# One more of 24 head pairs through TensorE in single precision, in an attention and gated-MLP kernel whose order of work is a searched table

## The chip, the cores and the metric

The kernel runs on one core of a Trainium2 chip. The metric is device time in microseconds (us) for one launch. Beside the timed runs one execution was recorded by the hardware profiler; all rows below come from that execution. Engines: PE is TensorE (its weight loads are PEld), DVE is VectorE, ACT is ScalarE, POOL is GpSimd, SP is SyncE, which here issues every DMA.

## The reference

Four batches of 12 heads, 448 tokens, 64 channels a head; then a gated MLP with a mixing step over tokens.

```python
scores = scale * np.matmul(q, k.transpose(0, 1, 3, 2))        # causal mask
attn = softmax(scores)
x = np.matmul(attn, v)                                        # heads side by side: 768 columns
h = np.maximum(x @ w_in, 0.0); u, v = h[..., :512], h[..., 512:]
v_s = np.einsum('ts,bsd->btd', w_spatial, layernorm(v)) + b_spatial[None, :, None]
out = (u * v_s) @ w_out
```

## The kernel before, in words

Two heads make a pair, so there are 24 pairs, six a batch. For each pair the kernel loads q and k, turns them so that the 64 channels lie on partitions, multiplies them (the scores), takes the row extreme with the mask (DVE, lines 970 and 1110), the exponential (ACT, 980 and 1129), the row sums and reciprocals, turns the weights, and multiplies by v (line 1255, into the bank `px`). After the sixth pair of a batch `ffn` runs the MLP on TensorE (line 1473).

There are two ways to do a pair, chosen by `TURNED` and `SINGLE`; both hold pairs 0 to 9 before the change.

**A turned pair** (`WIDE`) stays in single precision. q and k come by four loads, one for each of q, k and head (line 701). TensorE turns q and k (line 764, eight transposes) and ACT or DVE copies the result to `qkT`. `wide` makes the scores in three TensorE steps: heads 0 and 1 side by side on the upper and lower 64 rows (`both(0)`, `both(2)`, then `last()`; line 934, sixteen instructions in all). The weights are evened by one scaled copy each (line 1012, seven of them), turned by sixteen TensorE transposes (line 1021), and copied to `et` (seven copies, line 1050).

**A split pair** cuts every operand into a high and a low half-precision part. q and k come by two loads (line 708). ACT sums their squares (line 567), TensorE adds these over partitions (line 604), DVE makes a power of two of it, three engines make the parts (lines 513 to 521), a DMA transpose turns them (line 828), and two copies bring halves across partitions (line 847). The scores are 28 half-precision matmuls in four groups (lines 1101 and 1102). ACT makes the high part of the weights (line 1205), DVE the low part (line 1211), four DMA transposes turn them (line 1229), and the product with v takes three terms, 24 matmuls instead of 16 instructions.

**Pair 0** is turned in a form of its own (`HEADWISE`): line 738 turns q and k once for each head, four copies instead of two follow (lines 747 and 749), and the first four score steps are one head each (`one(g)`).

**Order.** Nothing is scheduled at run time. `Plan.add` numbers the steps in the order in which the Python code makes them. `ORDER` lists these numbers in the order in which they are issued, each engine taking its own from the list; `WHERE` has one letter for each step that may run on more than one engine. An engine works strictly in this order, so a step that waits holds up all behind it on its engine. `plan.run` puts short filler matmuls (line 689) on TensorE early on where it expects a wait. The buffers that tie engines together are four score banks `ps`, three `qk`, two `qkT`, two `e` and two `et`.

Of the kernel before, what the change touches and what calls it, by code (L numbers as in the profile page):

```python
# [12 lines left out]
AF = mybir.ActivationFunctionType  # L13
# [6 lines left out]
HEAD_PE = 690, 680  # L20
HEADWISE = frozenset({0})
# [4 lines left out]
TURNED = frozenset(range(10))  # L26

SINGLE = frozenset(range(10))
# [21 lines left out]
    "AAADAAPPADAPPAPPPAPAAPDAAPAAPPAAPDPAPADDAPAADAAAPAAAPADDDAADAADAPDDDPAADAAPPAAAPDAPAPDAAADPADAPADDPAPDAAPPAAPD"  # L50
    "AAPADAPADPAPAPAPPAPAPPPPPPPAPAPADPPDAPPADPDPAPAPAPPPPAADAAAPAAADPPPPAPAPAPDDAADAAAAPDAPPDAPAPAPDAAPPDDAADAPAPA"
    "PADDAADDDAADADDAAAAAPPADSSAAAAADPDAAAAAPAAPDAADDDPDAPDAPSSPPDPPAPPDPAAAPAAAAAPPPAPAPDDDDADDAADPAPPAPADPADPAAPP"
    "SPPPPPPPPDPADPPDPADPPPDPPDDPPPAPDDPAPPPPDAPPAAPPPAPAADAPPPPPPAPAPAAAAAAAADAAPPPPDDPDPPSPPPDDDAPSPAPPPDPPSSPAAP"
    "PDPPPPADPPDDPADPPDDAADADPPPADAPPDDAAADDDA"
)
ORDER = (
# [243 lines left out]
def kernel(  # L300
# [415 lines left out]
    def qk_turn(p):  # L716
# [3 lines left out]
        if not WIDE[p]:  # L720

            def clear(e):

                if not blank.get(at(t).name):
                    nc.gpsimd.memset(q32(at(t)), 0.0)
                    blank[at(t).name] = True

            plan.add({"POOL": 819}, clear, [], [(t, (0, 0)), (t, (0, 1))])
        if p in HEADWISE:
            pts = [Buf("ps"), Buf("ps")]  # L730
            for h in range(2):
                for n in range(2):
# [1028 lines left out]
```

## Time and profile before

| | |
|---|---|
| median of three timed runs | 358.56 us (358.33 to 358.65) |
| the profiled execution, its own time | 360.6 us |
| its span, first to last instruction | 358.6 us |
| granted TensorE clock over the span | 0.998 |
| PE, PEld, DVE, ACT, POOL busy | 97%, 63%, 80%, 75%, 45% |
| filler matmuls, line 689 | 32, 7.4 us busy |

The profiled execution lies 2.0 us above its span and 2.0 us above the median of the timed runs. A time is read here as a difference to the execution before. A busy share counts an engine as busy from the start of an instruction to its modelled end. In the chain of waits the time of a group of matmuls runs from its first start to the start of what follows.

### The profile page before, as it was taken

What the parts mean: (1) busy time and instruction counts of PE and PEld (TensorE: products, weight loads), DVE (VectorE), ACT (ScalarE), POOL (GpSimd) and SP (SyncE); (2) the same over time, 40 slices, a digit from 0 to 9 for tenths busy, and PEclk for the clock granted to TensorE, in tenths of its full rate; (3) what the DMA queues carried; (4) which work ended last, traced back from release to release, by engine and by line L of the source; (5) the groups of instructions that cost most, each with busy time, mean ns of one, the idle gap of its engine ahead of it and who ended that gap; (6) DMA issues with size and microseconds to landing.
All of it is one profiled execution on the core that took longest, in us unless ns stands there. A gap on an engine that the chain in (4) does not pass through costs nothing.

```text
span 358.6 us, 8098 instructions
## 1 busy us (share of the span) xinstructions
PE 346.2 (97%) x2602; PEld 225.5 (63%) x2602; DVE 285.9 (80%) x1116; ACT 268.7 (75%) x767; POOL 161.6 (45%) x223
## 2 busy tenths in 40 slices
PE   6999899999999999999999999999999999999995
PEld 5476555665555556765455579755755885555695
DVE  4899889999999999889898998987989994263420
ACT  3698899999999999888799989748789684231101
POOL 3133664337656468364374572334686710042400
PEclk9999999999999999999999999999999999999999
DMA  7959979746768999999997898997767978300014
GB/s 162 210 164 242 244 170 215 174 100 166 150 166 186 208 237 181 178 182 139 188 180 153 172 225 162 205 174 156 164 116 156 159 111 174 82 2 0 3 47 130
DMA packets 160796, 55.84 MB, mean 156 GB/s; under 512 B 155249, under 2 KB 156530, under 8 KB 160754
## 3 DMA queue, kind: packets, MB, share of 16 engines
q1 hardware_dynamic: 160754, 55.33, 74.5%
q8 instruction: 20, 0.33, 0.4%
q14 instruction: 22, 0.18, 0.1%
HBM read 26.76 MB, written 5.51 MB: 90 GB/s over the span
## 4 chain that ended last, share of the span: by engine, by line
PE 65%; DMA 10%; DVE 8%; ACT 7%; POOL 4%; issue 3%; SPq 2%; POOLq 0%; ACTq 0%; DVEq 0%
PE pf L1473 43%; PE px L1255 6%; DMA qkT<-qks 4%; PE ps L1021 3%; PE ps L934 3%; PE ps L1101 3%; ACT e L982 3%; PE ps L1102 2%; DMA et<-e 2%; PE ps L764 2%; POOL qks L523 2%; DVE ps L972 1%; DMA o<-in_moe_w_out_dram 1%; DMA wst<-wb 1%; ACT e L489 1%
## 5 line engine op out<-in xcount | busy, mean ns | idle before, releaser
L1473 PE MATMUL pf<-wi,xT 128*128 128x512 f16 (+1 forms) x360 | 61.6, 338 | 0.0
L1473 PE MATMUL pf<-xT,wi 128*128 128x448 f16 x288 | 59.3, 353 | 0.4 <-ACT hv L1536 0.4
L1124 ACT ACTIVATE ps<-ps,sm 128x384 f32<-128x384 f32 (+4 forms) x98 | 45.4, 463 | 13.2 <-DVE sm L1112 8.0
L1473 PE MATMUL pf<-wo,g 128*128 128x384 f32 x288 | 54.9, 341 | 0.0
L1213 DVE SCALAR_TENSOR_TENSOR e<-ps,sm,e 128x256 f16<-128x256 f32 (+4 forms) x98 | 46.3, 505 | 6.3 <-ACT e L489 6.3
L1473 PEld LDWEIGHTS pf<-wo,g 128*128 128x128 f32 x288 | 49.8, 188 | 2.0 <-issue 1.1
L489 ACT ACTIVATE e<-ps,sm 128x256 f16<-128x256 f32 (+4 forms) x98 | 44.3, 509 | 5.5 <-DVE sm L1146 1.9
L1112 DVE CUSTOM_DVE_ANT_0 ps<-ps,mask,sc 128x256 f32<-128x256 f32 (+4 forms) x98 | 47.2, 506 | 1.4 <-PE ps L1102 0.8
L1473 PEld LDWEIGHTS <-wi 128*128 128x128 f16 x288 | 27.4, 98 | 26.7 <-issue 3.0
L1473 PEld LDWEIGHTS <-xT 128*128 128x128 f16 (+1 forms) x360 | 27.2, 103 | 25.4 <-issue 4.7
L491 POOL TENSOR_SCALAR e<-e,sm 128x384 f32<-128x384 f32 (+3 forms) x43 | 23.8, 566 | 41.5 <-ACT e L982 13.6
L982 ACT ACTIVATE e<-ps,sm 128x256 f32<-128x256 f32 (+3 forms) x70 | 34.3, 500 | 4.6 <-DVE sm L972 2.6
L1473 PE MATMUL pf<-wst,vn 128*128 128x448 f16 (+1 forms) x176 | 36.0, 353 | 0.1
L523 POOL TENSOR_TENSOR qks<-qk,qks 112x512 f16<-112x512 f32 x21 | 24.2, 1157 | 20.3 <-ACT qks L489 8.9
L934 PE MATMUL ps<-qkT 64*128 64x128 f32 (+3 forms) x160 | 28.5, 444 | 0.9 <-ACT e L982 0.7
L1102 PE MATMUL ps<-qkT 128*64 128x256 f16 (+4 forms) x196 | 26.3, 284 | 0.4 <-DVE qkT L847 0.4
L1473 PEld LDWEIGHTS <-vn 128*128 128x128 f16 (+1 forms) x176 | 16.8, 98 | 15.2 <-issue 0.5
L1101 PE MATMUL ps<-qkT 128*64 128x256 f16 (+4 forms) x196 | 24.8, 291 | 0.9 <-DVE e L1213 0.7
L972 DVE CUSTOM_DVE_ANT_0 ps<-ps,e 128x128 f32<-128x128 f32 (+2 forms) x60 | 24.3, 441 | 1.2 <-PE ps L934 1.0
L1021 PE MATMUL ps<-ident,e 128*128 128x128 f32 x160 | 23.8, 279 | 1.3 <-POOL e L491 0.5
L1563 POOL TENSOR_TENSOR ln<-ln,mhalf 128x1 f32<-128x1 f32 (+1 forms) x16 | 10.6, 666 | 31.5 <-DVE ln L1555 26.8
L1021 PEld LDWEIGHTS ps<-ident,e 128*128 128x128 f32 x160 | 17.6, 141 | 9.1 <-issue 3.3
(168 smaller groups left out, 729.5 us busy)
## 6 DMA issues: line engine op xcount, KB each, us to landing
wb<-in_moe_w_in_dram SPq DMA_DIRECT2D x12, 512.0 KB, 4.3
vnat<-in_v_dram SPq DMA_DIRECT2D x24, 192.0 KB, 3.9
out_dram<-o SPq DMA_DIRECT2D x12, 384.0 KB, 3.0
qk<-in_k_dram SPq DMA_DIRECT2D x14, 224.0 KB, 4.0
qk<-in_q_dram SPq DMA_DIRECT2D x14, 224.0 KB, 4.2
o<-in_moe_w_out_dram SPq DMA_DIRECT2D x8, 384.0 KB, 4.1
qk<-in_q_dram SPq DMA_DIRECT2D x20, 112.0 KB, 4.8
qk<-in_k_dram SPq DMA_DIRECT2D x20, 112.0 KB, 3.6
```

What stands on the lines that cost most here:

```text
L489: nc.scalar.activation(out=dst, in_=src, func=AF.Copy, scale=scale)
L523: lambda e: HANDLE[e].tensor_tensor(out=dst_l(), in0=src(), in1=dst_h(), op=ALU.subtract),
L934: nc.tensor.matmul(out=at(bank)[r0:r0 + rn, o0:o0 + n], lhsT=flat32(t)[rows, q0:q0 + rn], rhs=k32(t)[rows, :n], start=True, stop=True, ski ...
L972: lambda e, ps=ps, n=n, u=u0 + u, sm=sm, o0=o0, h=h: nc.vector.tensor_tensor_reduce(out=at(ps)[:, o0:o0 + n], in0=at(ps)[:, o0:o0 + n], in ...
L982: lambda e, ps=ps, n=n, u=u0 + u, sm=sm, o0=o0, c=c: nc.scalar.activation(out=at(eb)[:, 128 * c:128 * c + n], in_=at(ps)[:, o0:o0 + n], fu ...
L1021: nc.tensor.transpose(out=at(pt)[:, 128 * i:128 * i + 128], in_=e32(at(eb))[:, c0 + i, :], identity=ident)
L1101: nc.tensor.matmul(out=o, lhsT=w, rhs=qkT[:, 2 + x, :n], start=True, stop=False)
L1102: nc.tensor.matmul(out=o, lhsT=w, rhs=qkT[:, 4 + x, :n], start=False, stop=True)
L1112: lambda e, ps=ps, n=n, u=u, sm=sm, o0=o0, m0=m0: nc.vector.tensor_tensor_reduce(out=at(ps)[:, o0:o0 + n], in0=at(ps)[:, o0:o0 + n], in1=m ...
L1124: nc.scalar.activation(out=dst, in_=src, func=AF.Exp, scale=-1.0, bias=at(sm)[:, u:u + 1], accum_out=at(sm)[:, 4 + 2 * u:5 + 2 * u],)
L1213: lambda e, part=part, src=src, sm=sm, u=u: nc.vector.scalar_tensor_tensor(out=part(1), in0=src(), scalar=at(sm)[:, 12 + u:13 + u], in1=pa ...
L1473: nc.tensor.matmul(out=o, lhsT=a(), rhs=rhs, start=(n0 + n == 0), stop=(n0 + n == len(mms) - 1), skip_group_check=len(out_ap()) > 1,)
```

## The change

Pair 10 becomes a turned pair. Pair 0 loses its own form: the head-by-head turns, copies and score steps are deleted, and it takes those of the other turned pairs. `WHERE` and `ORDER` are replaced (the plan has 2470 steps instead of 2496; only the first line of each table is shown). Constants and all other code stay.

```diff
-HEAD_PE = 690, 680
-HEADWISE = frozenset({0})
...
-TURNED = frozenset(range(10))
-
-SINGLE = frozenset(range(10))
+TURNED = frozenset(range(11))
+
+SINGLE = frozenset(range(11))
...
 WHERE = (
-    "AAADAAPPADAPPAPPPAPAAPDAAPAAPPAAPDPAPADDAPAADAAAPAAAPADDDAADAADAPDDDPAADAAPPAAAPDAPAPDAAADPADAPADDPAPDAAPPAAPD"
...
+    "DADPPDADAAPDPPAAPAPPADPAAAPPDDPAPAPAAAPAAAADADDAPAPADDDAADAADAADDDDAAPAAAAADAPDAPAAAPAAAPAADAPDDPAPAAAPPAAPDAA"
...
 ORDER = (
-    10, 1, 5, 0, 3, 73, 8, 6, 72, 100, 2, 75, 74, 4, 9, 14, 12, 11, 15, 96, 13, 26, 97, 22, 98, 93, 7, 16, 148, 18,
...
+    96, 11, 1, 0, 8, 4, 71, 5, 9, 10, 68, 3, 69, 7, 150, 2, 13, 12, 14, 70, 22, 15, 88, 92, 6, 73, 89, 93, 16, 18,
...
-        if p in HEADWISE:
-            pts = [Buf("ps"), Buf("ps")]
-            for h in range(2):
-                for n in range(2):
...
-        for g in range(4 if p in HEADWISE else 0):
...
-            if p in HEADWISE and n < 2:
-                continue
```

The numbers 10 to 13 are pair 0's loads (q of head 0, q of head 1, k of head 0, k of head 1) in both tables. Pair 1's loads are 72 to 75 before and 68 to 71 after. On TensorE the old table begins 14, 96, 98, 16, 18, 20, 101 (turn of pair 0, two of pair 1, three of pair 0, first scores of pair 0), the new one 14, 92, 16, 94, 97 (turns of pairs 0, 1, 0, 1, first scores of pair 0). The products with v come in the order of pairs 9, 10, 12, 11, 13 before and 9, 12, 11, 10, 13 after.

## Rows read from the trace of the kernel before

**Rows 1.** The page: busy time, share of the span, instructions of each engine.

```profile
PE 346.2 (97%) x2602; PEld 225.5 (63%) x2602; DVE 285.9 (80%) x1116; ACT 268.7 (75%) x767; POOL 161.6 (45%) x223
```

**Rows 2.** Stretches: length, then busy us of PE, PEld, DVE, ACT, POOL.

```profile
50.00:120.00 70.00, 69.40 (x518) 41.10 (x517) 66.03 (x268) 68.32 (x199) 38.88 (x54) 1.00 0.73 170
120.00:180.00 60.00, 57.65 (x450) 36.16 (x448) 53.78 (x220) 53.24 (x158) 30.63 (x39) 1.00 1.01 187
180.00:310.00 130.00, 129.97 (x1051) 88.43 (x1049) 108.69 (x433) 100.56 (x283) 61.67 (x72) 1.00 0.85 163
```

**Rows 3.** Waits of TensorE: total us, times, longest us.

```profile
PE ps L1101 <- DVE e L1213: 0.7, 2, 0.3
...
PE ps L1102 <- DVE qkT L847: 0.4, 1, 0.4
```

**Rows 4.** Chain of waits in order of time: start us, us, what.

```profile
50.59 0.77 PE ps L764 x8
51.36 1.42 PE ps L1021 x13
...
54.16 1.62 PE ps L934 x10
...
59.78 1.75 PE ps L934 x12
61.53 2.03 PE px L1255 x16
...
186.04 6.92 PE pf L1473 x36
...
196.64 0.34 PE px L604 x2
198.80 1.43 PE px L1255 x24
```

**Rows 5.** Timeline of PE: a split pair's first score matmuls, and what follows.

```profile
196.91 0.22 PE L1101 MATMUL ps<-qkT 128*64 128x64 f16 x2
...
198.63 1.54 PE L1255 MATMUL px<-et,vs 128*64 128x448 f16 x20
```

**Rows 6.** Timeline of PE: one group of scores between output matmuls.

```profile
141.07 2.35 PE L1473 MATMUL pf<-wo,g 128*128 128x384 f32 x12
143.35 0.38 PE L1101 MATMUL ps<-qkT 128*64 128x448 f16 x2
...
143.85 5.50 PE L1473 MATMUL pf<-wo,g 128*128 128x384 f32 x30
```

**Rows 7.** Timeline of PE: pair 0's last turn and first scores.

```profile
8.88 0.77 PE L738 MATMUL ps<-ident,qk 112*128 112x112 f32 x4
...
9.69 2.38 PE L934 MATMUL ps<-qkT 64*128 64x128 f32 x12
```

**Rows 8.** Timeline of ACT: a copy of a turned operand, and the first exponential.

```profile
8.40 0.53 ACT L785 ACTIVATE qkT<-ps 128x448 f32<-128x448 f32 x1
...
11.78 0.37 ACT L982 ACTIVATE e<-ps,sm 128x128 f32<-128x128 f32 x1 [2.29 <-DVE sm L972]
```

**Rows 9.** Timeline of SP: issue of the seventh and eighth load.

```profile
3.90 0.49 SPq L701 DMA_DIRECT2D qk<-in_q_dram  x1
4.43 0.49 SPq L701 DMA_DIRECT2D qk<-in_k_dram  x1
```

**Rows 10.** DMA issues up to 12 us: count, KB each, median us to landing.

```profile
qk<-in_k_dram SPq DMA_DIRECT2D x5, 112.0 KB, 3.0
```

**Rows 11.** Groups of ACT by line: count, busy us, mean ns, idle before.

```profile
L489 ACT ACTIVATE e<-ps,sm 128x256 f16<-128x256 f32 (+4 forms) x98 | 44.3, 509 | 5.5 <-DVE sm L1146 1.9 <-DMA et<-e 1.5 <-ACT ps L1124 1.4
...
L1045 ACT ACTIVATE et<-ps 128x384 f32<-128x384 f32 (+3 forms) x47 | 19.1, 446 | 1.7 <-PE ps L1021 1.3 <-DVE et L1047 0.3
```

**Rows 12.** Groups of DVE by line, the same columns.

```profile
L1213 DVE SCALAR_TENSOR_TENSOR e<-ps,sm,e 128x256 f16<-128x256 f32 (+4 forms) x98 | 46.3, 505 | 6.3 <-ACT e L489 6.3
```

**Rows 13.** Timeline of PE: pair 4's k turn waits for its load.

```profile
39.58 0.57 PE L764 MATMUL ps<-ident,qk 112*128 112x112 f32 x4 [1.01 <-DMA qk<-in_k_dram]
```

More of the change, by code (lines that the diff above doesn't have):

```diff
@@ L49 @@
 WHERE = (
-    "AAADAAPPADAPPAPPPAPAAPDAAPAAPPAAPDPAPADDAPAADAAAPAAAPADDDAADAADAPDDDPAADAAPPAAAPDAPAPDAAADPADAPADDPAPDAAPPAAPD"
[L51 to L54, printed above, removed]
+    "DADPPDADAAPDPPAAPAPPADPAAAPPDDPAPAPAAAPAAAADADDAPAPADDDAADAADAADDDDAAPAAAAADAPDAPAAAPAAAPAADAPDDPAPAAAPPAAPDAA"
+    "PDAAPADPDPAPAPDADADPPAPPPADAPAAPPDAAPADPDPAADPAPPPPAADAAAPAAAAPPPDAPAPPPDADDAADAPAAAAPAAPDPDPDAADPAAPPADAAPAPA"
+    "DDDAADPPDAAADAAAAAAAAAAAAADAAAPAADPADDDDPPAADPPDAPAADAAAPDADDSDPPDPAAPPPPPPPPADAAPPPPPDPPPPDDAADAAADAPADPSSPAA"
+    "PAAPDPPPDPPDPDDADPPPPPDPAAPPDPPSSAPPPPPDASPADDAAPAAPPAAPAAAAPPAPPPADPPAAAAAAAAPDPPSDPAPPPDPDPPPPPADPDSPPDPAPPS"
+    "DPDPPAPPSPPAAPPAPAADPAAPDDADPPAPPDADPDDAAAAAAD"
 )
 ORDER = (
[127 rows of a table removed]
[126 rows of a table added]
 )
@@ L728, in qk_turn @@
             plan.add({"POOL": 819}, clear, [], [(t, (0, 0)), (t, (0, 1))])
-        if p in HEADWISE:
-            pts = [Buf("ps"), Buf("ps")]
-            for h in range(2):
-                for n in range(2):
-                    rows = slice(64 * h, 64 * h + 64)
-                    def turn(e, n=n, h=h, rows=rows):
-                        src = at(s["qk"])[:, n].rearrange("p (c h) d -> p c (h d)", h=2)
-                        for c in range(NCH):
-                            nc.tensor.transpose(
-                                out=at(pts[n])[0:rows.stop, CP * c:CP * c + CP], in_=src[:, c, 0:rows.stop],
-                                identity=ident[:CP, :CP],
-                            )
-                    def copy(e, n=n, rows=rows):
-                        dst = (k32 if n else flat32)(at(t))[rows]
-                        blank[at(t).name] = False
-                        if e == "ACT":
-                            nc.scalar.activation(out=dst, in_=at(pts[n])[rows, :S], func=AF.Copy)
-                        else:
-                            nc.vector.tensor_copy(out=dst, in_=at(pts[n])[rows, :S])
-                    plan.add(
-                        {"PE": 386}, turn, [(s["qk"], (n, x)) for x in range(h + 1)] + [const_key("ident"), const_key("banks"), const_key("ones")],
-                        [(pts[n], 0), (t, "room")], cls="T",
-                    )
-                    plan.add({"ACT": c_act(S, "P"), "DVE": c_dve(S)}, copy, [(pts[n], 0)], [(t, (n, h))])
-            s["qkT_keys"] = [(t, (n, h)) for n in range(2) for h in range(2)]
-            return
         for n in range(2):
@@ L950, in wide @@
         whose = [(sums[g // 2], 2 * (g % 2) if g < 2 else g % 2) for g in range(5)]
-        def one(g):
-            for i in range(len(GROUPS[g])):
-                h, q0, n, o0, _ = GROUPS[g][i]
-                product(h, q0, n, banks[g], o0, 0, 128)
-        for g in range(4 if p in HEADWISE else 0):
-            plan.add(
-                {"PE": HEAD_PE[g // 2]}, lambda e, g=g: one(g),
-                [(s["qkT"], (n, g % 2)) for n in range(2)] + [const_key("banks")],
-                [(banks[g], u) for u in range(len(GROUPS[g]))] + [(eb, "room")], tail=70, cls="R",
-            )
         for n, fn in enumerate((lambda e: both(0), lambda e: both(2), lambda e: last())):
-            if p in HEADWISE and n < 2:
-                continue
             parts = [(banks[g], u) for g in (2 * n, 2 * n + 1) if g < 5 for u in range(len(GROUPS[g]))]
```

251 rows, old and new, of the table ORDER are left out of this document.

## The prediction

> **What bounds the kernel now.** I read the page first. TensorE is busy 97% of the span, no other engine above 80% [rows 1]. Such a share doesn't show whether one engine sets the end, so I cut the span into stages [rows 2]. From 180 to 310 us TensorE stands still for 0.03 us: there every microsecond of matmul counts in full. From 50 to 120 us it lacks 0.60 us and ACT is nearly as full (68.32 of 70 us); from 120 to 180 us it lacks 2.35 us, while ACT and DVE are at 89 and 90%. The list of waits says what it waited for: the low parts that DVE makes, and the copies across partitions, both of split pairs [rows 3]. Before 50 us TensorE is not the bound; there its fillers hide what it waits for. So work taken from ACT, DVE, POOL and SP can give back at most the idle of the middle (2.95 us) and something at the start; work added to TensorE costs its own length.
>
> **The change, part by part.** All terms are differences, worked out within the profiled execution; I put them on the median, 358.56 us.
>
> **Pair 10 on TensorE.** A turned pair: eight turns 0.77, sixteen transposes at 1.42/13, so 1.75, product with v 2.03 [rows 4]. Its scores are eight, four and four instructions: twelve of them took 1.62 (eight and four) and 1.75 (four and eight) [rows 4]. That makes 2.3 to 2.6 for sixteen, by how the first twelve are shared out; I take 2.5. Sum 7.05. A split pair: scores from 196.91 to 198.63, so 1.72 [rows 5], product 1.43, and the sum over partitions at most 0.34, the row of the same two-instruction step [rows 4]; I take 0.3. Sum 3.45. Pair 10 costs **3.6 us** more, between 3.3 and 3.9. Nothing covers it after 50 us.
>
> **Fewer changes of kind on TensorE.** I wrote out both tables by the numbering of the steps and counted unbroken stretches of one kind of TensorE work. Stretches of split scores go from 26 to 20; two of these were pair 10's. Stretches of single-precision scores go from 19 to 22, two of them pair 10's. What an isolated stretch costs is seen where one group of scores cuts the output matmuls: from 141.07 to 143.85 is 2.78 us for twelve output matmuls and four score matmuls [rows 6]. The thirty behind run at 5.50/30 or a little less, so twelve take 2.1 to 2.2. The rest, 0.6 to 0.7, is the group; in the dense scores its share by columns is 0.39 (1792 of 7936 columns of 1.72 us) [rows 5]. An isolated stretch thus costs about 0.27 us. Four fewer and one more are three fewer: **-0.8 us**. Bounds: zero (the gaps were idle that something else fills) and -1.6 (all six).
>
> **The start.** Before, TensorE turns pair 0's last operand until 9.65 and its first scores begin at 9.69 [rows 7]; the first exponential follows at 11.78 [rows 8]. The scores of head 0 stood behind the turn of head 1's k. After it, the seventh load is the last that pair 0 needs (k of head 0), and the eighth is the last of pair 1. SP issues them at 3.90 and 4.43 [rows 9], and such a load lands after 3.0 us [rows 10]: 6.9 and 7.4. Pair 0's k turn (0.77) ends at 7.7, pair 1's at 8.4; the copy (0.53) [rows 8] ends at 8.3. The scores can start at 8.45, 1.2 us earlier. Two copies and a pair of turns fewer stand before them. ACT, which paces the score stages that follow, would begin as much earlier: **-1.2 us**. Bounds: zero (a later wait takes it back) and -1.5. The eight loads are the same bytes in another order; SP is moved past none but these.
>
> **The other engines.** For pair 10, seven high parts on ACT (509 ns each, 3.6 us) [rows 11] and seven low parts on DVE (505 ns, 3.5 us) [rows 12] go, and five DMA transposes with their issue on SP. Added are seven copies (446 ns, 3.1 us) [rows 11], shared by ACT and DVE, and two copies of the turned q and k. The exponentials and mask steps stay seven each. The new letters give POOL 172 steps instead of 183 and ACT 199 instead of 186; five of ACT's thirteen more are pair 10's, eight lie outside it, at about 0.5 us each [rows 11] some 4 us in all. I cost that at nothing where ACT has room (180 to 310 us: 100.56 of 130 busy) and at up to 1 us if it falls between 50 and 120 us, where ACT has 1.7 us left [rows 2].
>
> **The idle of the middle.** In the new order pair 10's product stands behind those of pairs 12 and 11. So in the crowded stretch ACT and DVE have a split pair less ahead of them. The waits there (low parts, copies across) [rows 3] are of the kind that this shortens. I take **-2.5 us** of the 2.95 [rows 2]; bounds zero and -2.95. What is late next is TensorE itself.
>
> Sum: 3.6 - 0.8 - 1.2 - 2.5 = **-0.9 us**, 357.7 us. The terms nearly cancel, so the sign hangs on the last two.
>
> **The rivals.** *The middle's idle stays.* Engines work strictly in order, so a wait of TensorE depends on what stands next in its list, not on how full the others are. Pair 10's scores, transposes and product lie closely together in the new list, and between them ACT and DVE must do seven exponentials, evenings and copies. If they come late there, each wait holds up all of TensorE. Then the idle of 120 to 180 us is only moved: -0.9 + 2.5 = +1.6, 360.2 us. It turns slower than the measurement can miss once over 1.6 of the 2.5 us stay. For it: DVE and ACT are 89 to 90% full there [rows 2], and no single wait in these rows is above 0.4 us [rows 3], so the idle is spread and may not have one cause. Against it: the pair that goes is one of those waited for.
>
> *The loads pace the start.* Pair 4's k turn waits 1.01 us for its load [rows 13]; loads were issued as fast as before, so whoever comes earlier there only waits longer. Then the 1.2 us of the start are lost: +0.3, 358.9 us, no change to be seen. For it: that row. Against it: the order list gives these loads to SP behind steps of DVE and TensorE that also come earlier.
>
> *TensorE isn't full.* Its busy time runs to modelled ends, and weights were loading in only 63% of the span [rows 1]. If a third of its time were free, pair 10's 3.6 us would vanish: -4.5, 354.1 us. Against it: 36 matmuls in a row, with nothing to wait for and with their weights loading beside them, still take 6.92/36 = 0.19 us each [rows 4], and they are what fills the 130 us without a gap [rows 2]. The Trainium skill (Perfetto Trace Analysis, Identifying the Most-Contended Engine) calls matmul busy time a poor measure of the distance to the limit and wants the busy share of weight loads read instead; by that rule a third would be free. The row of the 36 matmuls disagrees here.
>
> **How the numbers follow.** A measurement of this kernel can tell about 0.2% (0.7 us) from no change. My forecast has a chance of 0.46, of which 0.36 below 357.84 and 0.10 just above. The idle that stays has 0.30 (0.28 slower, 0.02 same), the loads 0.20 (0.15 same, 0.03 slower, 0.02 faster), the free TensorE 0.04. Together: faster 0.42, same 0.27, slower 0.31. The forecast's own range is 356.5 to 358.6. With all bounds in its favour the sum is 3.3 - 1.6 - 1.5 - 2.95 = -2.75 (355.8); with the idle and the start both lost, +2.8 (361.4). I cut both a little, 356.0 to 360.9, and leave out 2 in 10.
>
> **What would show it.** First scores at about 8.4 us and first exponential about 1.2 us earlier show the start; pair 4's k turn then tells whether it lasts. TensorE's idle from 120 to 180 us should fall below 0.5 us. Lines 934 and 1021 should have 16 instructions more each, line 764 sixteen more (eight of them pair 0's), line 1229 four fewer. From 180 us on nothing but TensorE's sum should differ. I am wrong if TensorE waits about pair 10, or if its idle moves elsewhere after 50 us.

## The result, and the profile after

The changed kernel takes 360.84 us (median of five, 360.38 to 362.32), the kernel before 358.33 beside it. The ratio is 1.0069, 95% interval 1.0044 to 1.0094: **2.5 us slower**, where 0.9 faster was forecast. On another chip, later, it was 1.0047 (1.0024 to 1.0070), so 1.7 us slower. The 360.84 lies at the upper edge of the range, near the rival in which the middle's idle stays (360.2); but the trace shows another cause.

The profiled execution after takes 360.38 us, its span 358.6. That equals the span of the execution that the forecast started from, which was a long one: 2.0 us above the median of its kernel. A second execution of the kernel before, called *base* below, has a span of 357.1 us (its own time 359.07, still 0.6 above its median). I compare with that one: 1.5 us. One execution of a kernel differs from the next by as much as some of the effects here, so stage figures are checked below with a second execution of the changed kernel, *again* (span 359.7 us).

The page of the changed kernel, answering to [rows 1]:

```profile
PE 348.5 (97%) x2613; PEld 229.8 (64%) x2613; DVE 281.7 (79%) x1097; ACT 270.1 (75%) x769; POOL 147.8 (41%) x214
```

Stretches of the changed kernel, columns as in [rows 2], then clock, DMA share, GB/s:

```profile
120.00:180.00 60.00, 58.78 (x449) 38.49 (x446) 53.75 (x224) 52.48 (x158) 31.58 (x41) 1.00 0.95 190
180.00:310.00 130.00, 129.63 (x1063) 88.80 (x1062) 107.88 (x436) 101.28 (x287) 58.59 (x72) 1.00 0.84 157
```

And of *again*:

```profile
120.00:180.00 60.00, 58.08 (x434) 37.91 (x430) 53.49 (x221) 51.25 (x154) 31.49 (x41) 1.00 0.95 187
180.00:310.00 130.00, 129.33 (x1055) 88.54 (x1055) 108.61 (x438) 101.67 (x288) 58.72 (x72) 1.00 0.86 159
```

The same two stretches of base:

```profile
120.00:180.00 60.00, 58.13 (x454) 36.87 (x452) 53.86 (x221) 53.91 (x158) 31.19 (x39) 1.00 1.01 188
180.00:310.00 130.00, 129.96 (x1050) 88.37 (x1048) 108.58 (x432) 99.11 (x278) 60.56 (x70) 1.00 0.84 161
```

TensorE's idle from 120 to 180 us went from 1.87 us (2.35 in [rows 2]) to 1.22, and 0.33 of that came back behind 180 us. So the middle gave some 0.3 us against base, 0.8 against [rows 2], not 2.5. In *again* even that is missing: 1.92 us idle from 120 to 180 us and 0.67 behind, 0.7 more than in base. What the middle gave lies within what two executions of one kernel differ by.

The start went the wrong way. TensorE's timeline of the changed kernel, start and length in us, then count and the idle before (answers to [rows 7]):

```profile
4.78 0.98 PE L732 MATMUL ps<-ident,qk 112*128 112x112 f32 x4 [2.00 <-DMA qk<-in_q_dram]
...
6.94 1.48 PE L686 MATMUL pf<-ones 128*128 128x256 f16 x6
8.22 0.95 PE L732 MATMUL ps<-ident,qk 112*128 112x112 f32 x4
8.97 0.42 PE L686 MATMUL pf<-ones 128*128 128x256 f16 x1
9.18 0.95 PE L732 MATMUL ps<-ident,qk 112*128 112x112 f32 x4
9.93 0.42 PE L686 MATMUL pf<-ones 128*128 128x256 f16 x1
10.28 1.77 PE L902 MATMUL ps<-qkT 64*128 64x128 f32 x12
11.98 1.38 PE L686 MATMUL pf<-ones 128*128 128x256 f16 x11
```

And the changed kernel's first exponential on ACT:

```profile
12.57 0.47 ACT L937 ACTIVATE e<-ps,sm 128x256 f32<-128x256 f32 x1 [2.81 <-DVE sm L927]
```

The same places in base (first turn and first scores on PE, first exponential on ACT):

```profile
3.14 0.93 PE L738 MATMUL ps<-ident,qk 112*64 112x112 f32 x4 [1.29 <-DMA qk<-in_q_dram]
...
9.01 2.38 PE L934 MATMUL ps<-qkT 64*128 64x128 f32 x12
```

```profile
11.09 0.37 ACT L982 ACTIVATE e<-ps,sm 128x128 f32<-128x128 f32 x1 [1.79 <-DVE sm L972]
```

The first scores come at 10.28 us, not 8.45; the first exponential at 12.57, later than 11.78 [rows 8] and 11.09. Read the fillers: six take 1.48 us at 6.94, eleven take 1.38 us at 11.98. The same filler takes 0.21 us early and 0.11 later. The turns do likewise, 0.95 here and 0.55 to 0.60 later, each with its modelled tail. TensorE runs at half pace for its first ten microseconds, although the granted clock reads 1.00 (its upper level) from the first slice on.

Span is TensorE's work, its fillers and its idle. With the fillers taken off the busy time of the page (one profiled execution each, us):

| kernel | work | fillers and idle | span |
|---|---|---|---|
| base | 345.3 - 7.1 = 338.2 | 18.9 | 357.1 |
| pair 10 turned, pair 0 left (*apart*) | 347.7 - 7.6 = 340.1 | 17.5 | 357.6 |
| pair 0 in the common form alone (*heads*) | 346.5 - 10.4 = 336.1 | 22.0 | 358.1 |
| the change, both | 348.5 - 9.9 = 338.6 | 20.0 | 358.6 |

The spans here lie 0.5, 1.0 and 1.5 us above base, where the timed runs below say 1.5, 1.6 and 1.7 to 2.5; the table shows of what kind the parts are, not their full size. Pair 10 adds 1.9 us of work and takes 1.4 off fillers and idle. Pair 0's new form saves 2.1 us of work and loses 3.1: its fillers take 3.3 us more, and about as much idle goes at the start as comes back in the middle (57.10 us busy from 120 to 180 us in heads, 1.0 less than in base).

### The profile page after: what moved, and what is told of

It reads as the page before. It is cut to its first block, busy times and chain, and to the rows that moved or that the text cites. A ratio compares the mean times of both kernels' runs of the same rounds, so it can differ in the third digit from the quotient of the medians.

```text
span 358.6 us, 8079 instructions
## 1 busy us (share of the span) xinstructions
PE 348.5 (97%) x2613; PEld 229.8 (64%) x2613; DVE 281.7 (79%) x1097; ACT 270.1 (75%) x769; POOL 147.8 (41%) x214
## 4 chain that ended last, share of the span: by engine, by line
PE 62%; DVE 16%; ACT 8%; DMA 6%; issue 3%; POOL 3%; SPq 1%; ACTq 0%; POOLq 0%; DVEq 0%
PE pf L1428 40%; PE px L1210 6%; PE ps L902 5%; PE ps L976 3%; PE ps L1056 2%; ACT e L937 2%; PE ps L1057 2%; PE ps L732 2%; DVE ps L927 2%; DMA qkT<-qks 2%; ACT ps L1079 2%; POOL qks L520 1%; PE pf L686 1%; DMA o<-in_moe_w_out_dram 1%; DMA vnat<-in_v_dram 1%
## 5 line engine op out<-in xcount | busy, mean ns | idle before, releaser
L1079 ACT ACTIVATE ps<-ps,sm 128x384 f32<-128x384 f32 (+4 forms) x91 | 42.2, 465 | 9.6 <-DVE sm L1067 7.7
L1168 DVE SCALAR_TENSOR_TENSOR e<-ps,sm,e 128x256 f16<-128x256 f32 (+4 forms) x91 | 42.9, 504 | 3.7 <-ACT e L486 2.9
L1067 DVE CUSTOM_DVE_ANT_0 ps<-ps,mask,sc 128x384 f32<-128x384 f32 (+4 forms) x91 | 43.2, 507 | 2.9 <-PE ps L1057 2.2
L937 ACT ACTIVATE e<-ps,sm 128x256 f32<-128x256 f32 (+3 forms) x77 | 37.7, 501 | 6.2 <-DVE sm L927 4.8
L486 ACT ACTIVATE e<-ps,sm 128x384 f16<-128x384 f32 (+4 forms) x91 | 40.1, 517 | 1.9 <-DVE sm L1101 1.5
L902 PE MATMUL ps<-qkT 64*128 64x128 f32 (+3 forms) x176 | 31.2, 447 | 0.2 <-ACT e L937 0.2
L520 POOL TENSOR_TENSOR qks<-qk,qks 112x512 f16<-112x512 f32 x22 | 26.3, 1201 | 12.1 <-ACT qks L486 3.2
L927 DVE CUSTOM_DVE_ANT_0 ps<-ps,e 128x128 f32<-128x128 f32 (+2 forms) x66 | 26.8, 441 | 1.3 <-PE ps L902 1.1
L1057 PE MATMUL ps<-qkT 128*64 128x256 f16 (+4 forms) x182 | 23.7, 285 | 0.4 <-DMA qkT<-qkT 0.4
L1210 PE MATMUL px<-et,vnat 128*64 128x448 f32 (+3 forms) x176 | 23.0, 390 | 0.4 <-DVE xT L1232 0.4
L1056 PE MATMUL ps<-qkT 128*64 128x256 f16 (+4 forms) x182 | 22.6, 288 | 0.0
```

What stands on the lines that cost most here:

```text
L486: nc.scalar.activation(out=dst, in_=src, func=AF.Copy, scale=scale)
L520: lambda e: HANDLE[e].tensor_tensor(out=dst_l(), in0=src(), in1=dst_h(), op=ALU.subtract),
L902: nc.tensor.matmul(out=at(bank)[r0:r0 + rn, o0:o0 + n], lhsT=flat32(t)[rows, q0:q0 + rn], rhs=k32(t)[rows, :n], start=True, stop=True, ski ...
L927: lambda e, ps=ps, n=n, u=u0 + u, sm=sm, o0=o0, h=h: nc.vector.tensor_tensor_reduce(out=at(ps)[:, o0:o0 + n], in0=at(ps)[:, o0:o0 + n], in ...
L937: lambda e, ps=ps, n=n, u=u0 + u, sm=sm, o0=o0, c=c: nc.scalar.activation(out=at(eb)[:, 128 * c:128 * c + n], in_=at(ps)[:, o0:o0 + n], fu ...
L1057: nc.tensor.matmul(out=o, lhsT=w, rhs=qkT[:, 4 + x, :n], start=False, stop=True)
```

## The experiments

All are timed against the kernel before on the same chip; differences in us are the ratio times 358.5, with the 95% interval.

**The two executions compared.** *base* is the kernel before, unchanged.

> The kernel before, once more, for a second profiled execution: the first lay 2.2 us above the median of its timed runs, so its stages may show waits that the timed runs don't have. Theory A (the middle's idle belongs to this kernel): TensorE again idle by 2 to 2.5 us from 120 to 180 us, and the time 358.3. Theory B (that idle was that one execution's): the idle there below 1 us, the span about 356.5 us.

358.51 us, ratio 0.9999 (0.9987 to 1.0011); 1.87 us idle from 120 to 180 us, nearer to theory A. *again* is the changed kernel, unchanged, on the later chip.

> The changed kernel once more, on the same chip as the others: 2.0 to 2.9 us slower than before; first scores at 10.2 to 10.4 us.

+1.7 us (0.9 to 2.5); first scores at 9.86, a little earlier than expected: full pace came at 9.2 us in this execution.

**The halves of the change.** *heads*: the table of before, its steps renumbered.

```diff
-HEADWISE = frozenset({0})
+HEADWISE = frozenset()
```

> The kernel before with pair 0's heads together, pair 10 still split, and the old order: each new step stands where the later of the two head steps stood. Theory A (the start costs time when the heads go together, because pair 0's scores now wait for all its loads): first scores later than 9.69 us, time +0.5 to +1 us, 358.8 to 359.4. Theory B (heads together save TensorE time at the start): 357.3 to 358.3.

+1.6 us (0.9 to 2.2); first scores 10.15, first exponential 12.17. *apart*: the changed table, with pair 0's own form put back and the first 64 steps of the old order.

```diff
+HEADWISE = frozenset({0})
-TURNED = frozenset(range(10))
+TURNED = frozenset(range(11))
```

> The changed kernel with pair 0's heads apart again: the old form and the first 64 steps of the old order, then the new order; pair 10 stays turned. The plan's own costs give the same length for both forms. Theory A (the heads' form costs on the chip: no scores before the last turn and its copy, and more slow fillers ahead): first scores near 9.0 us instead of 10.3, time 359.0 to 359.8, 1 to 1.8 us below the changed kernel's 360.84. Theory B (a later wait sets the pace of the start): first scores early, time unchanged, 360.5 to 361.2.

+1.5 us (0.6 to 2.3); first scores at 9.26. That is only 0.2 to 1.0 us below the changed kernel, less than theory A had, and the two intervals overlap. Each half loses alone. Their sum, 3.1, is more than the 1.7 to 2.5 of both, within the intervals.

**The fillers at the start.** *nofill* is the changed kernel without those of 4.2 to 7.9 us of the plan's own clock; *later2* also puts pair 1's k turn behind pair 0's first scores.

```diff
-                if busy[e] < WARM and (2, []) in free["pf"]:
+                if busy[e] < WARM and not 4200 < busy[e] < 7900 and (2, []) in free["pf"]:
```

> The changed kernel without the filler matmuls that the plan puts between 4.2 and 7.9 us of its own clock (11 of 49), all else the same. Theory A (the start loses time because the fillers stand in front of turns whose loads have landed): pair 0's k turn starts at 6.8 instead of 8.22 us, its first scores at about 8.6 instead of 10.28, and the time falls by 1 to 1.7 us, to 359.1 to 359.8. Theory B (the start is paced by a later wait, on a load or on ACT): the first scores come earlier as well, but the time stays at 360.8.

> The changed kernel, with pair 1's k turn and its copy set behind pair 0's first scores in the table, and without the fillers of about 4.2 to 7.9 us. If the start's loss is the second turn and the fillers that stand ahead of the first scores, these come by 8.3 us or earlier, the first exponential at 11.0 or earlier, and the kernel gains 0.5 to 1.2 us on the changed one. If it is TensorE's slow pace in these 10 us, or the missing head-by-head form itself, the first scores come earlier but last longer, the first exponential is not before 11.5, and the time stays within 0.5 us of the changed kernel or above it.

nofill is +3.0 us (2.5 to 3.4) from before, later2 +3.4 (2.3 to 4.5): no gain on the changed kernel, although nofill's first scores come at 8.82 us and its first exponential at 11.64, 0.9 us earlier than there; by the first product with v behind 87 us that lead is gone (90.68 us against 90.23). TensorE's start in later2, two turns first, then the first scores:

```profile
4.51 2.09 PE L732 MATMUL ps<-ident,qk 112*128 112x112 f32 x8 [1.73 <-DMA qk<-in_q_dram]
7.09 0.98 PE L732 MATMUL ps<-ident,qk 112*128 112x112 f32 x4 [0.48 <-DMA qk<-in_k_dram]
8.70 1.65 PE L902 MATMUL ps<-qkT 64*128 64x128 f32 x8 [0.63 <-ACT qkT L753]
10.28 1.01 PE L732 MATMUL ps<-ident,qk 112*128 112x112 f32 x4
11.08 1.35 PE L686 MATMUL pf<-ones 128*128 128x256 f16 x7
```

The scores come 1.6 us earlier than in the changed kernel, but eight of them take 1.65 us, about what twelve took in *again* (1.57). The first exponential is at 12.96. Without the fillers TensorE stays at half pace until 11.9 us (12.3 in nofill). With the fillers that seemed to be in the way the slow pace ended some 2 us earlier (9.2 and about 10 us in the two executions of the changed kernel).

*fill* halves the other way: in the kernel before, fillers between 6 and 9 us count double for the plan, which leaves 29 of 32.

```diff
-                    while now + (fill := FILL if now > 6000 else 2 * FILL) < start - 40:
+                    while now + (fill := FILL if now > 9000 else 2 * FILL) < start - 40:
```

> The kernel before, counting a filler at its slow length (214 ns) until 9 us of the plan's clock instead of 6: three fillers fewer ahead of the first scores. Theory A (fillers hold up turns whose loads have landed): first scores 0.3 to 0.6 us earlier, time 357.9 to 358.4. Theory B (fewer fillers, later full clock): no earlier first exponential, time 358.5 to 359.0.

+0.1 us (-0.7 to 0.9): three fillers make no difference that shows.

**Work on TensorE, relief on the others.** *morepe* adds 3.6 us to TensorE in the kernel before, ahead of pair 10's product.

```diff
+            for _ in range(19 if p == 10 else 0):
+                nc.tensor.matmul(out=at(px)[:, 0:S], lhsT=wi[:, 0, 0, 0:128], rhs=wi[:, 0, 0, 0:S], ...)
```

> The kernel before with nineteen more matmuls of 448 columns (19 x 0.19 = 3.6 us, their result is overwritten) on TensorE ahead of pair 10's product with v: pair 10's extra TensorE time without anything taken off the other engines. Theory A (TensorE sets the end in the middle): +3.4 to +3.8 us, 361.7 to 362.1. Theory B (3.6 us partly vanish in waits that TensorE has there anyway): +1 to +2.5 us.

+2.2 us (1.5 to 2.8), so 1.4 of the 3.6 do not show. Its trace places 0.55 of that: TensorE's idle from 50 to 310 us is 1.98 us instead of 2.53 in base, and the wait for the copies across at 150 us [rows 3] is gone from its list. Where the rest went is not shown. *relief* leaves out pair 10's high and low parts and lets POOL clear the buffer; *swap* has both edits.

> The kernel before with pair 10's seven high parts on ACT (3.6 us) and seven low parts on DVE (3.5 us) left out; a memset of that buffer on POOL stands in their place, so pair 10's result is not attention. It shows what ACT's and DVE's relief is worth with nothing added to TensorE. Theory A (relief gives back most of the middle's idle): -1.2 to -2.2 us, 356.3 to 357.3, TensorE idle from 120 to 180 us below 1 us. Theory B (in-order waits stay): 358.0 to 358.7.

> Both together in the old order: 3.6 us of matmuls ahead of pair 10's product, and its high and low parts left out. It is the change to pair 10 without the new order and without pair 0's part. Theory A (the relief is worth its 2 us beside the added TensorE time too): 358.3 to 359.0. Theory B (the added TensorE time has already filled the idle, so relief has nothing left to give): 360.2 to 360.8, as with the added matmuls alone.

+1.6 (0.9 to 2.4) and +4.9 us (3.8 to 6.1). relief decides nothing, since POOL's clearing (2.65 us) stood ahead of an evening that TensorE waited 2.3 us for. Between the two, which share that fault, the added 3.6 us cost 3.3, or nearly all. *relief2* lets DVE clear the parts in short steps instead; *swap2* is that and the matmuls of morepe; *relief3* makes pair 10's transposes plain copies as well.

```diff
-                    lambda e, ...: scaled_copy("ACT", part(0), src(), at(sm)[:, 12 + u:13 + u]),
+                    lambda e, ...: None if p == 10 else scaled_copy(...),
-                    lambda e, ...: nc.vector.scalar_tensor_tensor(
+                    lambda e, ...: [nc.vector.memset(part(hl), 0.0) for hl in range(2)] if p == 10 else nc.vector.scalar_tensor_tensor(
```

> The kernel before, but pair 10's seven high parts on ACT (3.6 us) are left out and its seven low parts on DVE (3.5 us) become fourteen short memsets of the same buffer, so that DVE has no more to do than before and TensorE, the copies and the transfers stay as they are; pair 10's weights are zeros, so its share of the output is. Theory (work taken from ACT and DVE in the crowded middle gives TensorE's idle back): faster than before by 0.5 to 1.9 us, the idle of 120 to 180 us falling from 1.9 us to under 1.2. Rival (the idle stays): within 0.4 us of before, the idle still near 1.9.

> The same with nineteen 448-column matmuls (3.6 us) ahead of pair 10's product: both things that turning pair 10 does, with nothing else moved and the table of before. Theory: slower than before by 1.7 to 3.1 us, at least 0.5 us better than 3.6, and not worse than the 2.1 us that the matmuls cost without the relief. Rival: 3.2 to 3.8 us slower, the relief gives nothing back where TensorE is the bound.

> The kernel of relief2 (pair 10's high and low parts left out) with pair 10's four DMA transposes of the weights made plain copies as well: most of what turning pair 10 takes off ACT, DVE and the transfers, with nothing added on TensorE and nothing moved. Theory (transfers pace the middle): DVE waits no longer for the load of w_out there, and the kernel is 0.4 to 1.2 us faster than before. Rival: within 0.4 us of before, as relief2 was.

relief2: -0.2 us (-0.9 to 0.5); swap2: +2.2 (1.4 to 3.1), the same as morepe and 2.4 above relief2; relief3: +1.1 (0.4 to 1.8), slower than either of its expectations. Three times the relief gave nothing. In relief2, DVE's timeline shows a new wait, and TensorE's shows who waits for it:

```profile
122.32 0.36 DVE L1293 TENSOR_SCALAR hv<-o 128x384 int32<-128x384 int32 x1 [0.61 <-DMA o<-in_moe_w_out_dram]
```

```profile
122.93 0.55 PE L1021 MATMUL ps<-ident,e 128*128 128x128 f32 x3 [0.86 <-DVE e L487]
```

A lighter DVE reaches the unpacking of w_out before its load has landed: it waits 0.46 us at 118.59, where base does not wait. SP's issue of the next such load then takes 1.45 us (0.39 in base), and DVE waits again, as shown. The evening behind it in the list, for which TensorE waits, starts at 122.60 us instead of 121.47. Why that issue takes longer is not shown.

**The transfers.** *light* makes the sixteen DMA transposes of the weights of pairs 10 to 13 plain copies, in the kernel before.

```diff
+                        if 10 <= p <= 13:
+                            nc.sync.dma_start(out=e16(at(et))[:, o0 + f:o0 + f + m, :], in_=e16(at(es))[:, b0 + f:b0 + f + m, :])
+                            continue
                         nc.sync.dma_start_transpose(
```

> The kernel before, with the sixteen DMA transposes of the weights of pairs 10 to 13 (those of the crowded middle) made plain copies of the same tiles, so that these weights are not turned; every wait and every other step stays. The middle's DMA engines were busy 101% of 120 to 180 us by the profile's share. Theory (transfers pace the middle, and the idle that pair 10's turning won there came from its five transposes): the DMA share of 120 to 180 us falls under 0.9, TensorE's idle there from 1.9 us to under 1.2, and the kernel is 0.5 to 1.5 us faster than before. Rival (full DMA engines, but nobody waits for them): share falls, idle and time stay within 0.4 us.

-1.5 us (-2.0 to -0.9). Its middle stretch:

```profile
120.00:180.00 60.00, 59.24 (x465) 37.59 (x465) 55.67 (x224) 55.55 (x163) 32.93 (x40) 1.00 0.80 194
```

The DMA share falls from 1.01 to 0.80, TensorE's idle from 1.87 to 0.76. So lighter transfers of these weights free the middle. By which way is not shown: from 110 to 175 us the copies also land sooner themselves (median 2.7 to 3.7 us by size, the transposes 4.2), while the loads of w_out (3.9 us in base, 4.0 in light) and of v (4.1 in both) land as before. The share alone does not tell: in relief3 it is 0.95, and TensorE's idle is 2.39.

**Keeping TensorE at work before the first load.** *keep_a* gives the changed kernel nine more fillers at the first one, *keep_b* six to the kernel before, *heads_k* six to heads.

```diff
+        first = next(i for i, x in enumerate(order) if x[0] is self.warm)
+        order[first:first] = [(self.warm, "PE")] * 9
```

> The kernel before with six more fillers at its first one, 0.21 us each, so that TensorE stands still no more from 1.9 to 3.1 us while it waits for the first load. Theory (the start is paced by TensorE itself, which runs its matmuls at half pace until 7.6 to 9.3 us and takes the full pace the earlier the longer it has been kept at work): a filler falls from 0.21 to 0.11 us before 7 us, the first scores come at 8.6 us or earlier, the first exponential at 10.8 or earlier, and the kernel is 0.3 to 1.0 us faster than before if the start still counts at the end. Rival (loads pace the start, or what it gains is waited away behind it): the pace or the first scores come earlier, but the time stays within 0.3 us of before.

> The changed kernel with nine more fillers at its first one, so that TensorE works from 1.1 us to the first load's landing. Theory: the full pace comes before 8.5 us instead of 9.2 to 9.9, the first scores at 9.5 or earlier, and the kernel gains 0.4 to 1.2 us on the changed one (1.7 to 2.5 us slower than before without them). Rival: the pace comes earlier, but the time stays within 0.3 us of the changed kernel's 1.7 to 2.5.

> The kernel of heads (before, with pair 0 in the common form and pair 10 split) with six more fillers at its first one. It lost 1.6 us to before with its first scores at 10.15 us. Theory (the common form of pair 0 needs TensorE at full pace, because its four turns and four more scores stand ahead of the first exponential): first scores at 8.6 or earlier, first exponential at 10.6 or earlier, the time at most 0.3 us above before, and up to 1.0 below. Rival (the common form costs in itself, by the missing first head's scores): still 1 to 1.6 us slower than before.

keep_a: +0.3 us (-0.2 to 0.8) from before. Against the changed kernel's two measurements, taken on other chips, nine fillers return 1.4 to 2.2 us of the loss. TensorE's start in keep_a:

```profile
1.11 3.51 PE L688 MATMUL pf<-ones 128*128 128x256 f16 x16 [1.11 <-DVE ones L620]
4.72 0.57 PE L734 MATMUL ps<-ident,qk 112*128 112x112 f32 x4
...
7.42 0.55 PE L734 MATMUL ps<-ident,qk 112*128 112x112 f32 x4
7.80 0.27 PE L688 MATMUL pf<-ones 128*128 128x256 f16 x1
8.10 1.57 PE L904 MATMUL ps<-qkT 64*128 64x128 f32 x12
```

and its first exponential:

```profile
10.19 0.48 ACT L939 ACTIVATE e<-ps,sm 128x256 f32<-128x256 f32 x1 [2.14 <-DVE sm L929]
```

From 4.72 us on everything runs at full pace. The first scores come at 8.10 us, even before the forecast's 8.45, and the first exponential 2.4 us earlier than in the changed kernel. The lead lasts: the first product with v behind 87 us starts at 87.44 us, against 90.23 in the changed kernel and 89.55 in again.

keep_b: +0.4 us (-0.1 to 1.0), no gain. Full pace comes at 5.1 us instead of 6.7 to 9.3, but the last turn then waits 0.74 us for its load, and the scores start at 9.16: there the load paces the start.

heads_k: +2.0 us (1.3 to 2.8), no gain, although its first scores come at 8.74 and its first exponential at 10.76, 1.4 us earlier than in heads. The product of the first pair behind 88 us (88.13 us) is still 1.4 us ahead of heads (89.50) and 1.2 ahead of base (89.32). Then TensorE, DVE and ACT read:

```profile
119.92 1.29 PE L1017 MATMUL ps<-ident,e 128*128 128x128 f32 x7 [1.10 <-DVE e L1209]
...
137.22 1.62 PE L1251 MATMUL px<-et,vs 128*64 128x448 f16 x24 [1.62 <-DVE xT L1273]
```

```profile
118.36 0.58 DVE L1286 TENSOR_SCALAR hv<-o 128x384 int32<-128x384 int32 x1 [1.25 <-DMA o<-in_moe_w_out_dram]
```

```profile
134.55 0.63 ACT L485 ACTIVATE qks<-qk 112x512 f16<-112x512 f32 x1 [1.42 <-DMA qkT<-qks]
```

In the old table the start's gain is spent waiting in the middle: the first wait again stands behind a load of w_out, the second (1.62 us) behind a stretch in which ACT waits 1.42 us for a DMA transpose and DVE stands still too. In the new table most of the gain reaches the end.

*mend* is keep_a with three steps of the table moved, each ahead of a wait that it made (steps 936 before 1321, 701 before 1358, 1400 before 950).

> The kernel of keep_a with three steps moved in the table, each ahead of the wait it made for TensorE in that trace: the squares of pair 11's k ahead of three high parts of pair 12 on ACT (TensorE waited 0.84 us for them), one output copy of batch 0 ahead of small steps on DVE (0.66 us), and a mask step of pair 13 into DVE's 0.81 us wait for a transfer. Theory (TensorE's idle after 50 us is single waits that can be moved one by one): 0.6 to 1.5 us better than keep_a, so 0.3 to 1.2 below before, with the idle of 120 to 180 us under 0.5. Rival (each wait that goes makes another late): within 0.4 us of keep_a's 0.3 above before, with other waits of the same length in their place.

+0.8 us (0.1 to 1.5) from before, no better than keep_a. The idle of 120 to 180 us did fall, from 1.53 to 0.83 us in the two traces, and the waits of 0.84 and 0.66 are gone or 0.27. That such a gain reaches the end is not shown.

No version that computes the output beats the kernel before; keep_a equals it within the noise.

## Why the prediction was wrong

**The start** is the step that failed first: "The scores can start at 8.45, 1.2 us earlier". They came at 10.28 us, and at 9.86 in again. I added loads, turns and copies by their lengths, and took TensorE as free in between. The trace of before already showed more:

```profile
3.88 0.85 PE L689 MATMUL pf<-ones 128*128 128x256 f16 x3
...
7.92 0.95 PE L738 MATMUL ps<-ident,qk 112*128 112x112 f32 x4
8.67 0.42 PE L689 MATMUL pf<-ones 128*128 128x256 f16 x1
...
9.49 0.27 PE L689 MATMUL pf<-ones 128*128 128x256 f16 x1
```

Fillers stand in TensorE's list between the turns and are worked off in order, and until about 9.3 us turns and fillers take nearly twice as long as later. The 0.77 that I took for a turn [rows 7] lies between the two paces. The common form needs both heads' q before its first turn, so that comes at 4.78 us, after TensorE stood still for 2.00 us, instead of at 3.14 after 1.29 (base); half pace lasts until 9.2 or about 10 us. keep_a shows scores at 8.10 once the pace is there, worth 1.4 to 2.2 us in the new table. heads does not price the start: it is 1.6 us slower where -1.2 was forecast, but only 0.2 us behind base at 89 us, and heads_k, which leads base there by 1.2, still ends 2.0 slower. What the common form costs in the old table is lost behind that point, in waits of the middle. The bound of zero was the wrong end: nothing in the rows excluded a loss.

**The idle of the middle** was mis-sized: of the 2.5 us, 0.3 came in one execution and nothing in the other. With apart, the sum without the start says 3.6 - 0.8 - 2.5 = +0.3, and 1.5 was measured: about 1.2 us of the miss lie outside the start. keep_a, which has the forecast's start, leaves the same 1.2 (+0.3 where -0.9 was forecast). The other 1.4 to 2.2 us of the miss are the start's, all within intervals of 0.5 to 0.9 us to either side. I blamed ACT and DVE, 89 and 90% busy; but the DMA share in the same row [rows 2] reads 1.01, and I passed over it. relief2 takes ACT's 3.6 us away and gains nothing. light makes transfers lighter and gains 1.5. In the changed kernel the split pairs' small waits [rows 3] are gone, but from 120 to 180 us a wait for an output copy (0.85 us) and one for a part of x (0.35) stand in their place; in again a wait of 0.77 us for ACT stands beside these two. I had also sized the idle by the longer of two executions, 2.35 where base has 1.87.

**Pair 10's own 3.6 us** was too little where the pair stands. Its turns, scores, transposes and product in the changed kernel, PE, with what stands between:

```profile
154.85 0.99 PE L732 MATMUL ps<-ident,qk 112*128 112x112 f32 x8
155.77 0.52 PE L1428 MATMUL pf<-wi,xT 128*64 128x256 f16 x6
...
156.93 0.93 PE L902 MATMUL ps<-qkT 64*128 64x128 f32 x8
157.79 2.76 PE L1428 MATMUL pf<-wi,xT 128*128 128x512 f16 x12
...
160.60 1.96 PE L902 MATMUL ps<-qkT 64*128 64x384 f32 x8
162.49 0.82 PE L1428 MATMUL pf<-wi,xT 128*128 128x512 f16 x3
163.32 0.52 PE L976 MATMUL ps<-ident,e 128*128 128x128 f32 x3
163.77 1.62 PE L1210 MATMUL px<-et,vs 128*64 128x448 f16 x24
165.33 1.84 PE L976 MATMUL ps<-ident,e 128*128 128x128 f32 x13
167.09 0.28 PE L1056 MATMUL ps<-qkT 128*64 128x192 f16 x2
...
167.61 2.16 PE L1210 MATMUL px<-et,vnat 128*64 128x448 f32 x16
169.70 0.30 PE L1056 MATMUL ps<-qkT 128*64 128x256 f16 x2
```

From each start to the next, the turns take 0.92 us (0.77 forecast), the scores 0.86 + 1.89 = 2.75 (2.5), the transposes 0.45 + 1.76 = 2.21 (1.75), the product 2.09 (2.03). That is 0.9 us more than the sum had, with no wait shown: scores and transposes stand in two pieces each, and thirteen transposes take 1.76 here, 1.42 in [rows 4]. The net is another matter: over the whole run TensorE's work without fillers rises by 1.9 us in apart, less than the 2.8 that this term and the changes of kind make together. So the sum did not fail by too little work on TensorE. No wait stands about the pair, so that fear of the rival's was wrong. In morepe a lump of 3.6 us costs 2.2; "work added to TensorE costs its own length" was too strong in the middle.

**Fewer changes of kind** fit their size: the 1160 matmuls of the MLP take 221.8 us in base and 220.8 in the changed kernel, by the sum of their five rows, 221.6 to 221.8 in five more executions with the old table and 220.5 to 220.9 in six more with the new one. That is 1.0 us against 0.8; the gaps around the scores are not in it, and the rows run to modelled ends, so it supports the term rather than measures it.

**The rivals.** *The middle's idle stays* gave 360.2 us, close to the 360.84; that is in part luck, since it kept the start's -1.2, and the start lost instead. Its mechanism, other waits in place of those that go, is what the middle shows. *The loads pace the start* holds for keep_b, not for the change. *TensorE isn't full* had the added work at nothing, and fell: 3.6 us of matmul cost 2.2 (morepe), 2.4 (swap2 less relief2) and 3.3 us (swap less relief by the ratios, 3.7 by the medians).

What stays open: which transfers of the middle count and by which way (sixteen transposes made lighter gained 1.5 us, four of them, with pair 10's parts left out, lost 1.1), why light's relief pays where that of the engines does not, and why apart and heads together lose 0.6 to 1.4 us more than the change, a difference within the intervals.

## What to carry to other kernels

When a step at the start is made "earlier", read first how long the same small instruction takes there and later: here TensorE at half pace made fillers and turns nearly twice as dear. More fillers before the first load ended that early in all three kernels that had them, but the time fell in only one, so follow the lead to the end before counting on it. In a stage where TensorE waits, read every column of its row, the DMA share too, before an engine's work is blamed: in relief2, DVE with less to do waited for two loads that it does not wait for in base, and TensorE waited behind it. And where a term is below a microsecond, take a second execution of the same kernel before it is believed.

## What was not expected of the hardware

TensorE took 213 ns for a filler and 187 ns from one turn's matmul to the next at first, and 109 and 95 ns later, with the granted clock at 1.00 in all these stretches. The step came at 8.3 to about 10 us in apart, heads, again and the changed kernel, at 11.9 and 12.3 in later2 and nofill, which have fewer fillers, and before 5.2 us in the kernels kept at work from 1.1 or 1.5 us (5.4 in heads_k). In these, more work before the first load went with an early step, and fewer fillers with a late one.

That is not all that decides. Nine executions share the start of the kernel before (before, base, light, morepe, relief, relief2, relief3, swap, swap2). TensorE stood still for 1.17 to 1.36 us before the first turn in all of them, and yet the step came between about 6.7 us (morepe) and 9.3 (before); both of these waited 1.31 us. Two executions of the same program, base and before, differ there by 1.7 us, and their spans by 1.5. What else decides is not shown.
